# The V loads of an attention decode step, moved from SyncE's DMA queue to GpSimd's software queue

## The chip, the core and the metric

The kernel runs on one core of a Trainium2 chip. The metric is the time of one execution on the device in microseconds (us), the median of several runs; lower is better. A core has five engines that run side by side, each with its own instruction stream: TensorE (PE in the profile), VectorE (DVE), ScalarE (ACT), GpSimd (POOL) and SyncE (SP). Sixteen DMA engines move data between the memory of the chip and the core's on-chip memory; the instruction streams only issue the transfers.

## The reference

One decode step of attention for two sequences, gated by an MLP. All data are float32.

```python
def A(x, k_cache, v_cache, wq, wo):          # x [2, 1, 512]; caches [2, 32, 8192, 128]
    q = (x @ wq) split into 32 heads of 128
    scores = einsum("bhqd,bhkd->bhqk", q, k_cache) * 128 ** -0.5
    p = softmax(scores)
    o = einsum("bhqk,bhkd->bhqd", p, v_cache)
    return o joined over the heads @ wo      # wq [512, 4096], wo [4096, 512]

def B(x, w1, b1, w2, b2):
    return gelu(layernorm(x) @ w1 + b1) @ w2 + b2   # w1 [512, 1376], w2 [1376, 512]

xn = layernorm(x)
return x + A(xn, ...) * silu(B(xn, ...))
```

K and V together are 537 MB, each element of which is used once; the other inputs are 22 MB.

## The kernel before, in words

**Units.** The 64 pairs of sequence and head are taken two at a time: 32 units (n = 0 to 31). A unit needs 8.39 MB of K and as much of V, each laid out as 128 partitions of one contiguous row of 64 KB.

**Buffers.** There are three buffers of that size: two for K (`kb`, used in turn) and one for V (`vb`). They fill nearly all of the on-chip memory. `vb` is first used for the weights and scratch tiles of the MLP (the names in `boot`), and at the very end for `wo`; one of the `kb` first holds `wq`. The last unit's V goes into a K buffer, in two halves; K of the first and of the last unit come in two halves too.

**What a unit does.** VectorE multiplies K by the unit's query in two halves (L523, `scores_mul`, in place), sums the products over the 128 elements of a head in two halves (L530, `scores_sum`) and takes the maximum of each partition (L534). TensorE turns these maxima into a row (L537); VectorE takes the maximum of each of the two heads from it (L540, `max_dve`); TensorE spreads it again (L546), ScalarE copies it (L547) and computes the exponentials (L551) and a scaled column for the sums (L555). Then TensorE multiplies the exponentials with V in 32 steps (L574, `weighted`), ScalarE copies the sums (L581), TensorE folds them (L583) and VectorE writes them to the unit's columns of a table (L589, `spread`).

**The order of the units' work.** The loop at L594 writes the order out by hand for all engines, unit by unit, and each engine runs its own instructions in that order. For unit n it holds: first half of the multiply of n; the maximum of n-1 (L540) and its exponentials; second half of the multiply; `weighted(n-1)`; the load of V of n (`load_v`, L503); the sums and the maximum of n; `spread(n-1)`; the load of K of n+2 (`load_k`, L316). So on VectorE the maximum of unit n-1 stands behind the first multiply of unit n, and on SyncE, which issues both kinds of load, V of n stands ahead of K of n+2.

**The waits.** The class `Plan` records which instruction reads and writes which tile and puts the waits before the instructions. V of n waits until `weighted(n-1)` has read `vb`; K of n+2 waits until the sums of n (L530) have read its buffer. Every load has a semaphore for its kind and buffer. `load` (L313) issues all of them with SyncE's `dma_start`; only `x` (L339) is issued by ScalarE. The loads at the start are w1, w2, b1, b2, wq, K of unit 0 (two halves), K of unit 1 and V of unit 0; V of unit 0 waits until the MLP and the queries no longer need `vb`, K of unit 1 until `wq` has been used (L481). At the end `wo` comes in five pieces (L620) after the last use of `vb`, and is multiplied at L647 and L656.

**GpSimd** writes the identity matrix and three other constants at the start (L342 to L346) and has nothing else to do.

Of the kernel before, what the change touches and what calls it, by code (L numbers as in the profile page):

```python
# [21 lines left out]
class Plan:  # L22
# [18 lines left out]
    def op(self, eng, fn, r=(), w=(), over=(), it=None, loop=False, dma=None):  # L41


        o = Op()
        o.eng, o.fn, o.it, o.loop, o.dma, o.tell = eng, fn, it, loop, dma, False
        need = {}

        def after(d, war):
            if d.dma is None and dma is None and d.eng == eng and (eng == "pe" or war):
                return  # L50
            if d.dma is None:
                if need.get(d.eng) is None or need[d.eng].idx < d.idx:
                    need[d.eng] = d
            else:
                k = ("dma", d.dma)
                if need.get(k) is None or need[k].idx < d.idx:
                    need[k] = d

        for k in r:
            if k in self.writer:  # L60
                after(self.writer[k], False)
        for k in list(w) + list(over):
            if k in self.writer:
                after(self.writer[k], False)
            for d in self.readers.get(k, ()):
                after(d, True)
        clock = self.clock[eng]
        need = {k: d for k, d in need.items() if clock.get(k, 0) < d.idx}
        o.deps = [(k, d) for k, d in need.items()
                  if not any(e is not d and e.done.get(k, 0) >= d.idx for e in need.values())]  # L70
        for _, d in o.deps:
            for k, v in d.done.items():
                clock[k] = max(clock.get(k, 0), v)
        own = eng if dma is None else ("dma", dma)
        self.count[own] = o.idx = self.count.get(own, 0) + 1
        o.done = dict(clock)
        o.done[own] = o.idx
        for k in w:
            self.writer[k] = o
            self.readers[k] = []  # L80
        for k in r:
            if k not in w:
                self.readers.setdefault(k, []).append(o)
        self.ops.append(o)
# [80 lines left out]
def decode_kernel(nc, x, kc, vc, wq, wo, w1, b1, w2, b2, out):  # L165
# [31 lines left out]
    op = plan.op  # L197
# [13 lines left out]
    def sbuf(name, shape):  # L211
        return nc.alloc_sbuf_tensor(name, shape, F32).ap()
# [8 lines left out]
    vb = sbuf("vb", [P, KP * DH])  # L221
    kbuf = [t.rearrange("p (j d) -> p j d", d=DH) for t in kb]
    vbuf = vb.rearrange("p (j d) -> p j d", d=DH)
# [36 lines left out]
    boot = []  # L260
# [49 lines left out]
    vf = vc.rearrange("b h s d -> (b h s d)").rearrange("(n p j d) -> n p j d", p=P, j=KP, d=DH)  # L310
    M = KP // 2

    def load(dst, src, sem, w, over=()):  # L313
        op("sp", lambda: nc.sync.dma_start(dst, src), (), w, over=over, dma=sem)  # L314

    def load_k(n):  # L316
        i = (n + 1) % 2
        if n in (0, N - 1):
            for s in range(2):
                load(kbuf[i][:, s * M:(s + 1) * M], kf[n][:, s * M:(s + 1) * M], f"k{i}{s}", [("kb", i, s)])  # L320
            return
        load(kbuf[i], kf[n], f"kb{i}", [("kb", i, s) for s in range(2)])
# [4 lines left out]


    load(w1_sb, w1.rearrange("(p c) f -> p c f", p=P), "w1", ["w1"])
    load(w2_sb, w2.rearrange("f n -> (f n)").rearrange("(p e) -> p e", p=P), "w2", ["w2"])  # L330
    for t, src, k in ((b1_sb, b1, "b1"), (b2_sb, b2, "b2")):
# [169 lines left out]
    load_k(1)  # L501

    def load_v(n):  # L503
        load(vbuf, vf[n], "v", ["vb"], over=boot)

    load_v(0)

    def cols(t, a, n):
# [85 lines left out]
    for n in range(N):  # L594
        scores_mul(n, 0)
        if n:
            max_dve(n - 1)
            exps(n - 1)
        scores_mul(n, 1)

        if n:
            weighted(n - 1)
            if n < N - 1:
                load_v(n)
        scores_sum(n, 0)
        scores_sum(n, 1)
        max_rows(n)
        if n:
            spread(n - 1)

        if n + 2 < N:
            load_k(n + 2)
        elif n + 2 == N:
            for s in range(2):
                load(kbuf[1][:, s * M:(s + 1) * M], vf[N - 1][:, s * M:(s + 1) * M], f"v1{s}", [("kb", 1, s)])
# [80 lines left out]
```

## Time and profile before

| | |
|---|---|
| time, median of 3 runs | 1299.59 us (1299.52 to 1299.60) |
| span of the profiled execution, first to last instruction | 1298.3 us |
| moved by DMA | 559.39 MB, 431 GB/s over the span |
| VectorE busy | 1134.7 us (87%) |
| TensorE busy | 409.4 us (32%) |
| ScalarE busy | 77.6 us (6%) |
| GpSimd busy | 1.4 us |
| K load, issue to landing (median of 30) | 42.6 us |

The profile was taken in an execution of its own. Its span, 1298.3 us, runs from the first instruction to the last; the times of the runs contain what lies around that as well, and their median is 1.3 us longer. That table says who is busy, not who is waited for. For this the profile has a chain of waits (the work that ended last, followed back), a list of each engine's waits with what ended them, a timeline, and a table that gives each engine's busy time and the DMA engines' share in any stretch. An issue that waits in SyncE's stream shows as a wait of SPq, the queue of SyncE.

### The profile page before, as it was taken

Reading aid. Unit: us, or ns where it says so; the run is one execution under the profiler, and the core shown is the slowest. Engines: PE = TensorE matmul, PEld = TensorE weight load, DVE = VectorE, ACT = ScalarE, POOL = GpSimd, SP = SyncE. Lnnn points to the kernel's source line nnn. Section 1 sums busy time; section 2 is a strip of 40 time slices with the busy share of each in tenths; the row PEclk is TensorE's granted clock in tenths of the full one; section 3 lists DMA queues with packets and bytes.
Section 4 is the critical chain, followed back from the end, with each engine's and each line's share of the span. In section 5 each row is a group of like instructions: output and inputs, shape, how many; then the busy total and the mean of one; then the engine's idle time right before and its main releaser. Section 6 shows DMA issues by size and latency. Waiting matters only on the chain.

```text
span 1298.3 us, 6788 instructions
## 1 busy us (share of the span) xinstructions
PE 409.4 (32%) x2728; PEld 124.5 (10%) x2728; DVE 1134.7 (87%) x276; ACT 77.6 (6%) x250; POOL 1.4 (0%) x8
## 2 busy tenths in 40 slices
PE   5502333212333311333321333321333321333337
PEld 1100011000101000101100101000101100001103
DVE  3599989888889988889988888988888988888991
ACT  1100000000000000000000000000000000000000
POOL 0000000000000000000000000000000000000000
PEclk9856666556666556666555666655666655666659
DMA  9999999999999999999999999999999999999998
GB/s 406 445 423 444 424 436 436 426 444 426 440 428 430 440 426 444 424 436 436 426 444 426 440 428 434 438 424 444 426 434 436 426 444 426 440 428 434 423 436 360
DMA packets 10827, 559.39 MB, mean 431 GB/s; under 512 B 1208, under 2 KB 1216, under 8 KB 1476
## 3 DMA queue, kind: packets, MB, share of 16 engines
q1 hardware_dynamic: 10816, 559.30, 99.7%
q8 instruction: 4, 0.07, 0.0%
q14 instruction: 3, 0.02, 0.0%
q10 hardware_dynamic: 4, 0.00, 0.0%
HBM read 559.30 MB, written 0.00 MB: 431 GB/s over the span
## 4 chain that ended last, share of the span: by engine, by line
DMA 73%; PE 25%; DVE 1%; issue 0%; ACT 0%; SPq 0%; DVEq 0%
DMA vb<-in_A_v_cache_dram 71%; PE po L574 22%; DMA vb<-in_A_wo_dram 2%; PE s L409 1%; PE po L481 1%; PE s L451 0%; PE s L411 0%; PE acc L656 0%; DVE vb L417 0%; ACT L430 0%; DVE vb L355 0%; PE s L458 0%; SPq L314 0%; DVE vb L366 0%; DVE vb L443 0%
## 5 line engine op out<-in xcount | busy, mean ns | idle before, releaser
L523 DVE TENSOR_TENSOR kb<-kb,Q 128x8192 f32<-128x8192 f32 x64 | 555.6, 8681 | 106.3 <-DMA kb<-in_A_k_cache_dram 97.1
L530 DVE TENSOR_REDUCE sc<-kb 128x64 f32<-128x8192 f32 x64 | 552.3, 8666 | 0.0
L574 PE MATMUL po<-vb,PZ 128*8 128x512 f32 x1984 | 287.3, 744 | 296.4 <-DMA vb<-in_A_v_cache_dram 296.4
L546 PE MATMUL s<-nm,srow 1*128 1x2 f32 x64 | 18.4, 355 | 365.2 <-DVE nm L540 365.2
L574 PEld LDWEIGHTS po<-vb,PZ 128*8 128x8 f32 x1984 | 57.5, 104 | 500.2 <-issue 497.5
L537 PE MATMUL s<-ident,mx 128*1 128x128 f32 x32 | 11.8, 369 | 182.6 <-DVE mx L534 182.6
L546 PEld LDWEIGHTS s<-nm,srow 1*128 1x128 f32 x64 | 15.7, 302 | 374.5 <-DVE nm L540 374.5
L581 ACT COPY o<-po 128x512 f32<-128x512 f32 x32 | 18.7, 585 | 542.9 <-PE po L574 542.9
L547 ACT COPY bias<-s 128x2 f32<-128x2 f32 x32 | 5.1, 160 | 612.9 <-PE s L546 612.9
L583 PE MATMUL s<-mod,o 128*128 128x2 f32 x256 | 33.6, 253 | 22.1 <-ACT o L581 22.1
L583 PEld LDWEIGHTS s<-mod,o 128*128 128x128 f32 x256 | 31.1, 191 | 51.3 <-ACT o L581 51.3
L551 ACT ACTIVATE PZ<-sc,bias 64x128 f32<-64x128 f32 x64 | 25.5, 399 | 1.8
L537 PEld LDWEIGHTS s<-ident,mx 128*1 128x1 f32 x32 | 2.5, 79 | 186.1 <-DVE mx L534 155.5
L589 DVE TENSOR_TENSOR Z<-blk,s 128x8 f32 (+1 forms) x32 | 5.2, 163 | 12.4 <-PE s L583 12.4
L417 DVE COPY vb<-vb 2x384 f32<-2x384 f32 x4 | 1.8, 500 | 15.1 <-ACT vb L413 15.1
L551 ACT ACTIVATION_READ_ACCUMULATOR PZ<-sc,bias 64x1 f32 x64 | 11.8, 185 | 0.0
L409 PE MATMUL s<-vb 128*2 128x512 f32 (+1 forms) x24 | 11.7, 637 | 0.3 <-ACT vb L374 0.3
L665 DVE TENSOR_TENSOR gate<-acc,gate 128x128 f32<-128x128 f32 x1 | 0.3, 292 | 13.0 <-PE acc L656 13.0
L534 DVE TENSOR_REDUCE mx<-sc 128x1 f32<-128x128 f32 x32 | 9.2, 286 | 1.1
L555 ACT ACTIVATE ZR<-half,rs 128x8 f32 (+1 forms) x32 | 9.6, 301 | 4.1
L574 PE MATMUL po<-kb,PZ 128*8 128x512 f32 x64 | 8.7, 705 | 1.4 <-ACT PZ L551 1.4
L540 DVE TENSOR_REDUCE nm<-s 1x2 f32<-1x128 f32 x32 | 8.7, 272 | 0.3 <-PE s L537 0.3
(88 smaller groups left out, 83.8 us busy)
## 6 DMA issues: line engine op xcount, KB each, us to landing
kb<-in_A_k_cache_dram SPq DMA_DIRECT2D x4, 4096.0 KB, 43.3
kb<-in_A_v_cache_dram SPq DMA_DIRECT2D x2, 4096.0 KB, 40.5
vb<-in_B_w_dram SPq DMA_DIRECT2D x2, 2752.0 KB, 12.4
vb<-in_A_wo_dram SPq DMA_DIRECT2D x1, 4096.0 KB, 19.8
vb<-in_A_wo_dram SPq DMA_DIRECT2D x1, 2048.0 KB, 24.4
vb<-in_A_wo_dram SPq DMA_DIRECT2D x1, 1280.0 KB, 27.0
vb<-in_A_wo_dram SPq DMA_DIRECT2D x1, 512.0 KB, 27.7
vb<-in_A_v_cache_dram SPq DMA_DIRECT2D x31, 29.2
```

Of the source, the lines that this page charges most:

```text
L409: pe(lambda f=f, w=w, ph=ph, c=c: matmul(ph[:B, :w], yT[:, c, :], w1_sb[:, c, f:f + w], start=(c == 0), stop=False), ["yT", "w1"], [k])
L481: pe(lambda i=i, c=c, wv=wv, a=a, j=j, hd=hd: matmul(PO[R * j:R * j + NQ * B, :].rearrange("m (h d) -> m h d", d=DH), xnT[:, c, a:a + NQ * ...
L523: vector(n, n, lambda n: nc.vector.tensor_tensor(out=k, in0=k, in1=cols(Q, n * DH, DH).unsqueeze(1).to_broadcast([P, M, DH]), op=ALU.mult) ...
L530: vector(n, n, lambda n: nc.vector.tensor_reduce(out=SC[:, s * M:(s + 1) * M], in_=k, axis=AX.X, op=ALU.add), [("kb", i, s)], [("sc", s)])
L534: vector(n, n, lambda n: nc.vector.tensor_reduce(out=MX, in_=SC, axis=AX.X, op=ALU.max), [("sc", 0), ("sc", 1)], ["mx"])
L537: pe(lambda i: transpose(PM[:1, :P], MX, ident), ["mx", "ident"], ["s1"], it=n, loop=n > 0)
L546: pe(lambda i: matmul(PN[:, :U], srow, NM, start=True, stop=True), ["srow", "nm"], ["s2"], **one)
L551: act(lambda i, r=r, s=s: nc.scalar.activation(PZ[r, :, s, :], sc[r], AF.Exp, bias=BIAS[r, s:s + 1], scale=SCALE, accum_out=RS[r]), ["bias ...
L555: act(lambda i: nc.scalar.activation(cols(ZR, i * UP - UP, UP), half, AF.Copy, scale=RS), ["half"] + [("rs", s) for s in range(U)], [("ZR" ...
L574: pe(lambda i, t=t, j=j, v=v: matmul(PO[R * j:R * j + U * JW, :], PZ[:, t].rearrange("p s j -> p (s j)"), v[:, t * JW:(t + 1) * JW, :].rea ...
L581: act(lambda i: nc.scalar.copy(O4, PO), ["po"], ["o4"], **one)
L583: pe(lambda i, k=k: matmul(PT[:, :U], O4[:, k * DH:(k + 1) * DH], mod[:, k:U * JW:JW], start=(k == 0), stop=(k == JW - 1)), ["o4", "mod"], ...
```

## The change

V of units 0 to 30 is issued by GpSimd, over the queue whose descriptors a program on GpSimd writes (the software queue), instead of by SyncE over a hardware queue. `single_packet=True` asks that all that one DMA engine gets of such a load (eight rows of 64 KB) form one packet. The conditions of each load are the same as before; they stand in GpSimd's stream now. All K loads, the two halves of V of unit 31, the weights and `wo` stay on SyncE, in the order that they had among themselves. Nothing else differs; lines below the change move down by three.

```diff
-    def load(dst, src, sem, w, over=()):
-        op("sp", lambda: nc.sync.dma_start(dst, src), (), w, over=over, dma=sem)
+    def load(dst, src, sem, w, over=(), pool=False):
+        if pool:
+            op("pool", lambda: nc.gpsimd.dma_start(dst, src, single_packet=True), (), w, over=over, dma=sem)
+        else:
+            op("sp", lambda: nc.sync.dma_start(dst, src), (), w, over=over, dma=sem)
...
     def load_v(n):
-        load(vbuf, vf[n], "v", ["vb"], over=boot)
+        load(vbuf, vf[n], "v", ["vb"], over=boot, pool=True)
```

## Prediction

> **What bounds the kernel now.** I read the page's head first, its picture of the DMA engines and its queue table: 16 DMA engines at "9" in all but the last of 40 slices, and one queue, SyncE's, that fills 99.7% of their time.
>
> ```profile
> span 1298.3 us, 6788 instructions
> ...
> PE 409.4 (32%) x2728; PEld 124.5 (10%) x2728; DVE 1134.7 (87%) x276; ACT 77.6 (6%) x250; POOL 1.4 (0%) x8
> ...
> DMA  9999999999999999999999999999999999999998
> ...
> q1 hardware_dynamic: 10816, 559.30, 99.7%
> ```
>
> Then one unit in the middle of the run, from the table of stretches; the waits of SyncE's queue; and two neighbouring pieces of the chain of waits.
>
> ```profile
> 587.90:626.60 38.70, 10.73 (x75) 3.32 (x75) 35.03 (x8) 2.03 (x7) 0.00 (x0) 0.63 1.00 434
> ```
> ```profile
> SPq L314 <- PE po L574: 980.5, 31, 33.0
> SPq L314 <- DVE mx L534: 227.0, 31, 36.5
> ```
> ```profile
> 598.45 8.77 PE po L574 x64
> ...
> 637.14 9.90 PE po L574 x64
> ```
>
> From one V's first matmul to the next it is 637.14 - 598.45 = 38.7 us; in that unit the DMA share is 1.00 at 434 GB/s, while VectorE (third busy column) works 35.03 us. TensorE holds V's only buffer for some 9 us of it, and the DMA engines don't rest then: K is moving. Two equal loads, K and V of 8.39 MB, fill the unit, so one load takes 38.7 / 2 = **T = 19.35 us**, and each of the 8 rows of 64 KB that an engine carries of it (128 partitions over 16 engines) 2.42 us. The kernel is bound by the bytes. What a change adds is time in which the DMA engines have nothing to move; what it can save is their 0.3% of rest, at the ends.
>
> How the order in SyncE's queue keeps them busy stands in the timeline of that stretch, SyncE's issues first, then VectorE and one row of ScalarE (start, duration, engine, line; in brackets the idle time before).
>
> ```profile
> 607.24 0.33 SPq L314 DMA_DIRECT2D vb<-in_A_v_cache_dram  x1
> 613.82 0.33 SPq L314 DMA_DIRECT2D kb<-in_A_k_cache_dram  x1
> 647.06 0.33 SPq L314 DMA_DIRECT2D vb<-in_A_v_cache_dram  x1
> ```
> ```profile
> 617.84 8.69 DVE L523 TENSOR_TENSOR kb<-kb,Q 128x8192 f32<-128x8192 f32 x1 [3.64 <-DMA kb<-in_A_k_cache_dram]
> 626.45 0.27 DVE L540 TENSOR_REDUCE nm<-s 1x2 f32<-1x128 f32 x1
> 626.65 8.67 DVE L523 TENSOR_TENSOR kb<-kb,Q 128x8192 f32<-128x8192 f32 x1
> 635.25 17.26 DVE L530 TENSOR_REDUCE sc<-kb 128x64 f32<-128x8192 f32 x2
> 652.54 0.29 DVE L534 TENSOR_REDUCE mx<-sc 128x1 f32<-128x128 f32 x1
> 652.78 0.16 DVE L589 TENSOR_TENSOR Z<-blk,s 128x8 f32 x1
> ```
> ```profile
> 628.41 0.18 ACT L551 ACTIVATION_READ_ACCUMULATOR PZ<-sc,bias 64x1 f32 x1
> ```
>
> When V is issued at 607.24, the K load ahead of it has 617.84 - 607.24 = 10.6 us to go. That K lands, VectorE starts on it, V follows (637.14), then the K issued at 613.82. Every load queues behind one under way, and the half-finished one is always completed first.
>
> For later: VectorE's unit is 652.78 + 0.16 - 617.84 = **35.1 us**. From a unit's first multiply to the weights of the unit before (its maximum, L540, stands behind that multiply) it is 628.41 + 0.18 - 617.84 = **10.8 us** with the hand-over. TensorE holds V for 647.06 - 637.14 = 9.92 us here and for 607.24 - 598.45 = 8.79 before, mean **9.36 us**.
>
> **The change part by part.** 31 V loads leave SyncE's queue (0.33 us of issue each, off the path) and become 31 DMA instructions on GpSimd, which has nothing else left to do (8 instructions, 1.4 us in all). Bytes and compute stay. The waits stay too, but no longer in one line: K(n+2) isn't issued behind V(n), nor does V(n) move behind K(n+1). So the price hangs on how a DMA engine shares its time between two queues. The trace shows that in one place, the start.
>
> ```profile
> 0.73 0.87 SPq L314 DMA_DIRECT2D vb<-in_B_w_dram  x2
> ...
> 0.89 0.54 ACTq L339 DMA_DIRECT2D vb<-in_A_x_dram  x1
> ...
> 5.23 0.62 DVE L361 BATCH_NORM_STATS2 vb<-vb 2x6 f32<-2x512 f32 x1
> ```
> ```profile
> vb<-in_B_w_dram SPq DMA_DIRECT2D x2, 2752.0 KB, 12.4
> ```
>
> x (4 KB, ScalarE's queue) is issued after w1 and in use at 5.23. w1's 2752 KB at 434 GB/s take 6.5 us, so w1 was not through before 7.2. x got in between w1's rows: a hardware queue's load can be cut at a row, and then the other queue has its turn. By this a V whose eight rows are one packet waits for the K row under way, then has the engines for 19.35 us, while **K(n+1), half done, stands**. The sum is made for that. The Trainium skill ("DMA: Bandwidth & Descriptors", Queues, rings and completion order) says that an engine takes its queues in turn and changes only at the end of a packet; by that V runs through uncut, as here. It also calls packets of 9 to 17 descriptors typical, by which a K load might be one packet too and nothing would be reordered: rival 2. x among w1's rows speaks against that.
>
> *The software queue's delay* **L** (V issued to V moving, and its last byte to TensorE's start) isn't in the trace. The nearest row is the store at the end, on the hardware queue and nearly without bytes:
>
> ```profile
> 1296.51 0.66 SPq L667 DMA_DIRECT2D out_dram<-gate  x1
> ```
> ```profile
> 1.16 0.29 POOL L343 TENSOR_SCALAR_AFFINE_SELECT ident<-ident 128x128 f32<-128x128 f32 x1 [0.23 <-POOL ident L342]
> ```
>
> From its issue to the span's end it is 1298.3 - 1296.5 = 1.8 us, the lower end. The upper end is x's 5.23 - 0.89 = 4.3 us, which holds a row's wait. I take the nearer row and one small GpSimd instruction (0.29) on top: L = 2.1 us. The same page of the Trainium skill puts the software queue's first byte 0.4 us behind the hardware queue's; by that L would be 2.2 and the sum 1 us more.
>
> *Steady state.* Let an odd unit's multiply start at 0, its K just landed, the next K buffer full or taken. The weights of the unit before are ready at 10.8; its V, in place since long, is read until 20.2; there the next V is issued, and it moves 2.1 us later. The DMA engines have meanwhile moved one K (19.35 from 0) and then had nothing: both K buffers full, V's being read. They rest 20.2 + 2.1 - 19.35 = **2.9 us**. VectorE is through at 35.1 and a K is issued, which starts when V is done. The even unit's V is ready 35.1 us after the odd one's, so 35.1 - 19.35 = 15.75 us into that K; it cuts it with 3.6 us to go (a row begun and one whole) and delays it by 19.35. VectorE waits for it some 10 us, and then starts an odd unit again; this wait costs nothing more, the engines move bytes in it. A pair of units takes 2 x 38.7 + 2.9. Units 3 to 30 are 14 pairs: 14 x 2.9 = **+41 us**.
>
> *Start.*
> ```profile
> 45.66 0.43 SPq L314 DMA_DIRECT2D vb<-in_A_v_cache_dram  x1
> ```
> ```profile
> 47.74 17.38 DVE L523 TENSOR_TENSOR kb<-kb,Q 128x8192 f32<-128x8192 f32 x2 [8.24 <-ACT Q L496]
> 65.03 17.27 DVE L530 TENSOR_REDUCE sc<-kb 128x64 f32<-128x8192 f32 x2
> ```
> w1, w2, wq and K0 (22.4 MB, 51.6 us at 434 GB/s) are in at about 54. V0, issued at 45.66, now cuts in ahead of K0's second half, which comes at 54 + 19.35 = 73.4; unit 0 ends at 73.4 + 8.7 + 17.3 = 99.4 instead of 65.03 + 17.27 = 82.3, and K2 is issued there. K1 is in at 93, so the engines rest 7 to 8 us. V1 is issued at 99.4 + 20.2, again some 1.5 us late: together **+10 us**.
>
> *End.*
> ```profile
> 1268.16 0.29 DVE L534 TENSOR_REDUCE mx<-sc 128x1 f32<-128x128 f32 x1
> ```
> ```profile
> 1285.50 3.66 PE L647 MATMUL wide<-vb,on 128*17 128x512 f32 x32 [0.47 <-DMA vb<-in_A_wo_dram]
> 1290.40 1.94 PE L647 MATMUL wide<-vb,on 128*17 128x512 f32 x16 [1.25 <-DMA vb<-in_A_wo_dram]
> 1293.49 1.31 PE L656 MATMUL acc<-vb,on 128*17 128x128 f32 x40 [1.15 <-DMA vb<-in_A_wo_dram]
> ```
> Now unit 31's maximum is done early and the end waits for wo, last at 1293.5. V30 will cut ahead of K31's second half; after that half only V31 and wo (8.39 MB each, 38.7 us) remain, so it lands at 1293.5 + 41 + 10 - 38.7 = 1305.8. Then come 8.7 + 17.3 us of VectorE, and from the maximum on the stretch of now without its waits for wo (0.47 + 1.25 + 1.15): 1298.3 - 1268.2 - 2.9 = 27.2. The span ends at 1359.0, which is 1359.0 - 1298.3 - 51 = **+10 us** more.
>
> Sum: 1298.3 + 41 + 10 + 10 = 1359; the median of the runs, 1299.59, lies 1.3 us over this span, so **1361 us**.
>
> **Rivals.** *1. The packet isn't kept whole* (the change doesn't do what it says): rows of V and K take turns. A V beside a whole K takes 15 rows and L, 36.3 + 2.1; TensorE 9.36; the next V meets a K that has moved alone for 11.5 us, 19.35 + 7.9 + 2.1; TensorE 9.36: 86.5 us a pair, 9.1 over 77.4. 14 x 9.1 and some 3 at the start: **1430 us** (1414 to 1446, since TensorE's 8.8 to 9.9 counts twice a pair). For it: x and w1 took turns. Against: V's rows are asked for as one packet.
>
> *2. On the other side: K's loads can't be cut.* If a load of 64 KB rows holds an engine to its end, V waits for K(n+1) as now and still comes ahead of K(n+2): 10.6 us of cover against L. Price nothing, **1299.6**, if at the start K1 goes ahead of V0; with V0 first, K1 lands at 93 and the engines rest once, some 4 us: 1303. It decides where an engine is committed to 10.6 us of K, over four rows. x's place speaks against it, though w1's rows are a third as long.
>
> *3. V comes too late to cut.* The margin is 3.6 - 2.42 = 1.2 us, and TensorE's times differ by as much from V to V: in some units K finishes first and the rest falls away. Half of them would make it 1340; it lies in the range.
>
> *4. VectorE holds up GpSimd.* If descriptors could be written only between two VectorE instructions, each V issued at 20.2 would wait for the reduction that ends at 26.1: 14 x 5.9 more, **1444 us**. The Trainium skill ("SBUF — State Buffer", SBUF: two separate sides) has such a lock for VectorE's two-port modes; L523's 8192 elements in 8.69 us, less than one a nanosecond, don't look like one.
>
> **How the numbers follow.** Forecast 0.55, with rival 3 from 1335 to 1392 (L from 1.8 to 4.3: 1357 to 1392; TensorE at 8.8 or 9.9: 8 us either way); rival 1 0.20; rival 2 0.10, half of it no change; rival 4 0.05; 0.10 for what I don't see, of it 0.03 faster and 0.01 the same. Faster has only the 0.3% of rest to live on. The range that leaves out 2 in 10 is 1330 to 1445: forecast, rival 1 and rival 4. Within 0.2% (2.6 us), about what a measurement of this kernel can tell from no change: 0.06; faster 0.03; slower 0.91.
>
> **What would show it.** The page's table of DMA issues gives the time from a V's issue to its landing now:
>
> ```profile
> vb<-in_A_v_cache_dram SPq DMA_DIRECT2D x31, 29.2
> ```
>
> Right: a GpSimd queue with 260 MB beside the hardware queue's 299; V issued to landed in some 21 to 24 us instead of 29.2; VectorE waiting for K every second unit, some 10 us; DMA rests of 3 us at every second unit. Rival 1: V in 29 to 38 us, and TensorE waiting for V. Rival 2: VectorE's wait at 3.6 us a unit as now, DMA at "9" throughout. Wrong altogether: V's rows slower than 2.42 us, or GpSimd issuing V well after TensorE's last matmul on it.

## The result, and the profile after

| | time, median | runs |
|---|---|---|
| before | 1299.57 us | 1299.52 to 1299.60 (4) |
| changed | 1441.09 us | 1440.65 to 1442.87 (4) |

The ratio is 1.1092, 95% interval 1.1078 to 1.1105: 141.5 us slower, where 61 us were forecast. The sign and the cause in the large (DMA engines at rest between loads) were forecast; the way to it was rival 1's, not the forecast's. The time lies inside the stated range, 1330 to 1445 us, only because that range was drawn wide enough to hold rivals 1 and 4. The time alone can't tell these two apart (1430, up to 1446, and 1444 us); the traces and runs below do.

From the page after, the lines that answer to those of before:

```profile
span 1439.3 us, 6789 instructions
...
PE 397.9 (28%) x2728; PEld 122.5 (9%) x2728; DVE 1136.4 (79%) x276; ACT 77.7 (5%) x250; POOL 18.0 (1%) x39
...
DMA  9999999989979899798899988898989898899995
...
q1 hardware_dynamic: 6352, 299.25, 49.3%
q0 software_dynamic: 4464, 260.05, 41.8%
```

VectorE's and TensorE's busy times are as they were. The DMA engines are not: 49.3 + 41.8 = 91.1% of 1439.3 us is 1311 us with a packet on, against 99.7% of 1298.3, 1294 us, before. So of the 141 us that the span grew, 128 - 4 = **124 us are rest**, and 17 us are packets that took longer.

V's time from issue to landing, and TensorE's wait for V (before, after), are the signs that the prediction had named:

```profile
vb<-in_A_v_cache_dram POOLq DMA_DIRECT2D x31, 33.6
```
```profile
PE po L574 <- DMA vb<-in_A_v_cache_dram: 296.4, 31, 13.5
PE po L577 <- DMA vb<-in_A_v_cache_dram: 638.5, 30, 27.8
```

The landing's median was 29.2 us before. The forecast had 21 to 24 us for it, rival 1 had 29 to 38 and TensorE waiting for V. Both of rival 1's signs are there.

One V load in the middle, its TensorE work and the next, from the chain of waits; then VectorE's timeline and the issues of K and V in the same stretch:

```profile
634.19 32.61 DMA vb<-in_A_v_cache_dram
666.80 0.12 issue
666.92 9.89 PE po L577 x64
676.82 0.28 issue
677.10 34.65 DMA vb<-in_A_v_cache_dram
```
```profile
635.80 0.16 DVE L592 TENSOR_TENSOR Z<-blk,s 128x8 f32 x1 [9.96 <-PE s L540]
635.95 8.69 DVE L526 TENSOR_TENSOR kb<-kb,Q 128x8192 f32<-128x8192 f32 x1
...
670.66 0.29 DVE L537 TENSOR_REDUCE mx<-sc 128x1 f32<-128x128 f32 x1
678.68 0.16 DVE L592 TENSOR_TENSOR Z<-blk,s 128x8 f32 x1 [7.74 <-PE s L540]
```
```profile
670.65 0.33 SPq L317 DMA_DIRECT2D kb<-in_A_k_cache_dram  x1
```

V's issue to the next V's issue is 42.9 us here, and 43.5 on average from unit 2 to unit 30; before it was 38.7 on average (38.1 or 39.8 from one to the next). V takes 32.6 and 34.7 us to land here; V's landing and TensorE's work on it make up the whole unit, since the next V needs the same buffer. VectorE stands idle 10 and 8 us at the end of these two units ahead of L592, the small write of V's result, because that V is late (the bracket names TensorE's L540, which TensorE runs behind V's last step). Held there, VectorE starts the next unit late, and the K load that needs this unit's buffer is issued late, at 670.65.

What the DMA engines do between the V issue at 634.19 and that K issue is shown by the table of queues, in three stretches: 634.2 to 638.9, 641.5 to 655.9, and 666.5 to 671.5.

```profile
DMA packets 32, 2.10 MB, mean 446 GB/s; under 512 B 0, under 2 KB 0, under 8 KB 0
## 3 DMA queue, kind: packets, MB, share of 16 engines
q1 hardware_dynamic: 32, 2.10, 103.1%
```
```profile
q1 hardware_dynamic: 48, 3.15, 50.4%
q0 software_dynamic: 48, 3.15, 50.4%
```
```profile
DMA packets 0, 0.00 MB, mean 0 GB/s; under 512 B 0, under 2 KB 0, under 8 KB 0
```

In the first stretch K alone moves, two rows on each of 16 engines, though V has been issued. In the second both queues move the same, three rows each per engine. In the third nothing moves: V's last row is in, and the next K is issued only at 670.65. Laid end to end by their times in the trace, the 64 KB packets of each of the 16 engines from 626.5 to 666 us read the same (k is a row of K, V one of V):

```
kkkkkVkVkVkVVVVV
```

In this stretch V's rows are not run through together while K has rows left. A whole unit's rows are there, 16 x 2.42 = 38.7 us, and then the rest.

### The profile page after: what moved, and what is told of

Read it like the earlier page. It is cut to its first block, busy times and chain, and to the rows that moved or that the text cites. A ratio compares the mean times of both kernels' runs of the same rounds, so it can differ in the third digit from the quotient of the medians.

```text
span 1439.3 us, 6789 instructions
## 1 busy us (share of the span) xinstructions
PE 397.9 (28%) x2728; PEld 122.5 (9%) x2728; DVE 1136.4 (79%) x276; ACT 77.7 (5%) x250; POOL 18.0 (1%) x39
## 3 DMA queue, kind: packets, MB, share of 16 engines
q1 hardware_dynamic: 6352, 299.25, 49.3%
q0 software_dynamic: 4464, 260.05, 41.8%
## 4 chain that ended last, share of the span: by engine, by line
DMA 74%; PE 23%; issue 2%; ACT 0%; DVE 0%; SPq 0%; DVEq 0%
DMA vb<-in_A_v_cache_dram 70%; PE po L577 20%; DMA kb<-in_A_k_cache_dram 3%; DMA vb<-in_B_b_dram 1%; PE po L484 0%; PE s L412 0%; PE s L454 0%; PE wide L650 0%; PE s L564 0%; PE s L414 0%; PE s L586 0%; PE acc L659 0%; DVE vb L420 0%; ACT PZ L554 0%; PE s L426 0%
## 5 line engine op out<-in xcount | busy, mean ns | idle before, releaser
L577 PE MATMUL po<-vb,PZ 128*8 128x512 f32 x1984 | 282.4, 733 | 639.8 <-DMA vb<-in_A_v_cache_dram 638.5
L592 DVE TENSOR_TENSOR Z<-blk,s 128x8 f32 (+1 forms) x32 | 5.2, 163 | 236.1 <-PE s L540 217.6
L586 PE MATMUL s<-mod,o 128*128 128x2 f32 x256 | 33.6, 253 | 22.1 <-ACT o L584 22.1
L315 POOL DMA_DIRECT2D vb<-in_A_v_cache_dram x31 | 16.6, 535 | 1352.2 <-PE po L577 1261.0
L540 PE MATMUL s<-ident,mx 128*1 128x128 f32 x32 | 9.0, 282 | 67.1 <-DVE mx L537 67.1
L554 ACT ACTIVATE PZ<-sc,bias 64x128 f32<-64x128 f32 x64 | 25.5, 399 | 1.8
L543 DVE TENSOR_REDUCE nm<-s 1x2 f32<-1x128 f32 x32 | 8.7, 272 | 0.0
L540 PEld LDWEIGHTS s<-ident,mx 128*1 128x1 f32 x32 | 2.7, 85 | 68.2 <-issue 35.9
## 6 DMA issues: line engine op xcount, KB each, us to landing
vb<-in_A_v_cache_dram POOLq DMA_DIRECT2D x31, 33.6
```

Source lines behind the costliest of these rows:

```text
L315: op("pool", lambda: nc.gpsimd.dma_start(dst, src, single_packet=True), (), w, over=over, dma=sem)
L540: pe(lambda i: transpose(PM[:1, :P], MX, ident), ["mx", "ident"], ["s1"], it=n, loop=n > 0)
L554: act(lambda i, r=r, s=s: nc.scalar.activation(PZ[r, :, s, :], sc[r], AF.Exp, bias=BIAS[r, s:s + 1], scale=SCALE, accum_out=RS[r]), ["bias ...
L577: pe(lambda i, t=t, j=j, v=v: matmul(PO[R * j:R * j + U * JW, :], PZ[:, t].rearrange("p s j -> p (s j)"), v[:, t * JW:(t + 1) * JW, :].rea ...
L586: pe(lambda i, k=k: matmul(PT[:, :U], O4[:, k * DH:(k + 1) * DH], mod[:, k:U * JW:JW], start=(k == 0), stop=(k == JW - 1)), ["o4", "mod"], ...
```

## The experiments

**Theory 1**: an engine gives two queues one row each by turns, whether one packet was asked for or not and whatever the kind of queue. V lands late, VectorE waits for it, the next K is issued late, and the engines rest. **Theory 2**: the software queue is slow. **Theory 3**: the request for one packet holds rows together at least partly. Where a control is named, the run is read against it.

**Without the request for one packet.**
```diff
-            op("pool", lambda: nc.gpsimd.dma_start(dst, src, single_packet=True), (), w, over=over, dma=sem)
+            op("pool", lambda: nc.gpsimd.dma_start(dst, src), (), w, over=over, dma=sem)
```


> The changed kernel without the request for one packet (single_packet left out). Theory 1 (the DMA engines give the two queues one 64 KB row each by turns, whatever the request): nothing changes, 1434 to 1448 us, V's issue to landing 33 to 34 us. Theory 3 (the request does hold part of V's rows together): V's rows are cut up more, and the time moves by more than 1%.

Measured: 1445.28 us (ratio 1.112, 1.1102 to 1.1139), V's landing 33.7 us. The intervals of the run with the request and of this one touch; the request does nothing that can be told here.

**K on the software queue, V on the hardware queue.**
```diff
-        load(vbuf, vf[n], "v", ["vb"], over=boot, pool=True)
+        load(vbuf, vf[n], "v", ["vb"], over=boot)
...
-        load(kbuf[i], kf[n], f"kb{i}", [("kb", i, s) for s in range(2)])
+        load(kbuf[i], kf[n], f"kb{i}", [("kb", i, s) for s in range(2)], pool=True)
```


> Swapped queues: K of units 1 to 30 over GpSimd's software queue, V over SyncE's hardware queue. Theory 1 (turns between any two queues): 1415 to 1450 us, V lands 31 to 35 us after its issue as in the changed kernel. Theory 2 (the software queue itself is slow, some 4.4 us per load: its descriptors, its issue): V is quick again, K has more time to spare, and the time falls to 1300 to 1360 us.

Measured: 1447.56 us (1.1138, 1.1116 to 1.1161). The page's table of issues of this run:

```profile
vb<-in_A_v_cache_dram SPq DMA_DIRECT2D x31, 34.3
kb<-in_A_k_cache_dram POOLq DMA_DIRECT2D x30, 34.2
```

V is as late over the hardware queue as over the software queue, and the time is not the 1300 to 1360 us of theory 2. Two queues cost this, whichever of them V is in.

**Everything in the one software queue**, in SyncE's old order (K from unit 1 on, V, and wo).
```diff
-            load(kbuf[i], kf[n], ...)   # the same for K's halves of unit 31, V's halves, and wo
+            load(kbuf[i], kf[n], ..., pool=True)
```


> Every load from K of unit 1 on (K, V, wo) over GpSimd's one software queue, in SyncE's old order. Theory 1: with one queue there is nothing to take turns with, and the order of before is back: 1299 to 1305 us. Theory 2 (slow software queue): 62 loads at some 4.4 us or more, 1441 us or above.

Measured: 1306.85 us (1.0046, 1.0028 to 1.0064), 2 us over the range expected. Two stretches of it, the first 100 us and the steady part (DMA share and GB/s are the last columns):

```profile
0.00:100.00 100.00, 37.40 (x193) 10.43 (x193) 48.80 (x54) 12.14 (x25) 3.12 (x11) 0.74 0.95 403
237.24:1227.45 990.21, 284.33 (x1894) 85.73 (x1898) 899.51 (x182) 52.17 (x181) 27.44 (x52) 0.61 1.00 433
```

In the steady part the software queue keeps the engines at 1.00 and 433 GB/s, just as SyncE's queue did before in that stretch. The 7 us are lost at the start, where the first stretch has a share of 0.95 (before 0.99): V of unit 4 is issued at 227.82, before at 220.87, and the profiled span is 8.1 us longer (1306.4 us), so only 1 us is lost after that. K of unit 0 is still in SyncE's queue there, beside the loads of GpSimd's; that this is what costs the 7 us was not tried by itself. With one queue the order is back, and all but 7 of the 141 us are gone. That is far from theory 2's 1441 us or above: theory 2 falls.

**VectorE's write of V's result moved** behind the next unit's first multiply (the table Z gets one unit of columns in front, so that the loop stays regular).
```diff
         scores_mul(n, 0)
         if n:
+            spread(n - 2)
             max_dve(n - 1)
...
-        if n:
-            spread(n - 1)
```


> The changed kernel, with VectorE's small write that needs V's result (spread of unit n-1) moved behind the first multiply of unit n+1, so that VectorE no longer waits for V at the end of a unit. Theory 1 (V's late landing costs time because VectorE waits for it and so issues the next K late, while the DMA engines rest): most of the loss goes, 1318 to 1350 us. Rival (the alternation itself makes the transfers slower): 1425 to 1445 us.

Measured: 1372.01 us (1.0557, 1.0536 to 1.0578): half of the loss goes, 69 us, not most of it, and the time is 22 us over the range expected. The alternation alone would have left it at 1425 or more, so the wait is real; that the rest stays has its reason in VectorE's own list of waits:

```profile
DVE Z L592 <- PE s L540: 143.0, 17, 12.7
```

VectorE still waits in about every second unit (17 times), now behind the first multiply. The row names L592, which stands there directly ahead of the maximum of the unit before (L543); the transpose for that maximum, L540, stands on TensorE behind all 32 steps on V. V's lateness reaches VectorE by this way too; my expectation had left that out.

> Control: the kernel before with VectorE's write of V's result moved behind the next unit's first multiply. V is in time there, so nothing should change: 1298 to 1302 us.

The same edit of the kernel before: 1299.57 us (1.0000, 0.9989 to 1.0011). The edit is worth nothing by itself.

**K in four loads, rows of 16 KB.**
```diff
-        load(kbuf[i], kf[n], f"kb{i}", [("kb", i, s) for s in range(2)])
+        for r in range(4):
+            a = r * KP // 4
+            load(kbuf[i][:, a:a + KP // 4], kf[n][:, a:a + KP // 4], f"kb{i}{r}", [("kq", i, r)],
+                 over=[("kb", i, r // 2)])
...
-            [("kb", i, s)] + qs, [("kb", i, s)])
+            [("kb", i, s), ("kq", i, 2 * s), ("kq", i, 2 * s + 1)] + qs, [("kb", i, s)])
```


> The changed kernel with K of units 1 to 30 in four loads each, so that SyncE's rows are 16 KB and V's on GpSimd's queue stay 64 KB. Theory 1 (one row each by turns, whatever its size): V gets four fifths of each engine while K is there, lands in 22 to 28 us instead of 33.6, and the time falls to 1310 to 1365 us. Rival (the two queues share by bytes or by time, or the software queue is slow): V still lands after 33 to 34 us, 1430 to 1450 us.

> Control: the kernel before, with K of units 1 to 30 in the same four loads each, all on SyncE's queue. All theories: 1299 to 1304 us, so that what the run with quarter rows on two queues shows comes from the sharing.

Measured: 1317.98 us (1.0147, 1.013 to 1.0164); the control 1306.71 (1.0056, 1.0036 to 1.0076), 3 us over the range expected, so four loads of short rows cost 7 us by themselves and the second queue 11. Its row for V in the table of issues, and its steady part:

```profile
vb<-in_A_v_cache_dram POOLq DMA_DIRECT2D x31, 28.5
```
```profile
237.00:1227.00 990.00, 281.03 (x1890) 84.53 (x1894) 889.02 (x181) 52.12 (x181) 13.20 (x25) 0.61 1.00 431
```

V lands 5 us sooner (28.5, half a us outside what was expected), the engines are at 1.00 again, and the time is 123 us shorter; against the control, 130 of the 141 us are gone. While both queues have rows, the trace has one for one: from 625.5 to 635 us each queue starts 48 packets, V's of 64 KB and K's of 16 KB. But the edit does more than shorten K's rows. Each quarter of K is now a load with a wait of its own: two quarters of a K are issued when half of the sums that free the buffer are done (581.48 and 581.85, the other two at 590.07 and 590.44), and VectorE begins a unit when half of its K is in. So V's earlier landing goes with the shorter turns, but how much of the 123 us is due to them and how much to the earlier K was not separated.

**V in pieces of 16 KB**, as one packet and not.
```diff
-            op("pool", lambda: nc.gpsimd.dma_start(dst, src, single_packet=True), (), w, over=over, dma=sem)
+            op("pool", lambda: nc.gpsimd.dma_start(dst, src, single_packet=True, max_dma_last_dim=16384), (), w, over=over, dma=sem)
```

The second run has `max_dma_last_dim=16384` alone.

> The changed kernel with each V row cut into four pieces of 16 KB, still one load and one packet per engine asked for; K's rows stay 64 KB. Theory 1 (a turn is one piece of a load, the request for one packet does not hold pieces together): V gets one fifth of an engine while K is there, lands after 36 to 44 us on a median, 1435 to 1475 us. Theory 3 (the request holds, but only pieces under 64 KB): V runs through uncut, lands in 21 to 25 us, 1340 to 1385 us.

> The same with V's rows cut into pieces of 16 KB, without the request for one packet. Theory 1: as with the request, within 1%: 1435 to 1475 us. Theory 3: 1435 to 1475 us too, that is 5% or more above the run with the request.

Measured: 1466.46 us (1.1285, 1.1262 to 1.1308) with the request, 1467.56 (1.1293, 1.1271 to 1.1316) without: the same. Theory 3 falls for small pieces too. The times are in the range expected; V's landing is not, 33.6 and 32.4 us against the 36 to 44 expected. K, with four fifths of each engine, lands in 25.5 us instead of 33.9, and V has the engines alone after that. While both have pieces left, each queue gets as many turns as the other, with the request for one packet in place (655 to 673.5 us, V's queue is q0):

```profile
q1 hardware_dynamic: 96, 6.29, 78.4%
q0 software_dynamic: 96, 1.57, 19.8%
```

**K in pieces of 4 KB**, so that V gets nearly all of an engine: what the forecast had assumed.
```diff
-            op("sp", lambda: nc.sync.dma_start(dst, src), (), w, over=over, dma=sem)
+            op("sp", lambda: nc.sync.dma_start(dst, src, max_dma_last_dim=cut), (), w, over=over, dma=sem)
...
-        load(kbuf[i], kf[n], f"kb{i}", [("kb", i, s) for s in range(2)])
+        load(kbuf[i], kf[n], f"kb{i}", [("kb", i, s) for s in range(2)], cut=4096)
```


> The changed kernel with K's rows of units 1 to 30 cut into pieces of 4 KB (one load each, as before), so that V gets 16 of 17 turns by bytes while K is there: nearly what the forecast assumed, V through uncut. V should land 23 to 26 us after its issue. If the forecast's sum was right apart from that premise: 1345 to 1375 us plus what the control loses. If a V that comes early does little harm, as with quarter rows: 1305 to 1330 us plus what the control loses.

> Control: the kernel before with K's rows of units 1 to 30 cut into pieces of 4 KB, all on SyncE's queue. 1300 to 1330 us, by what small pieces cost; the run with the 4 KB pieces on two queues is read against this one.

Measured: 1378.50 us (1.0608, 1.0577 to 1.0638); the control 1333.41 (1.0261, 1.0231 to 1.029), 3 us over the range expected. Here only the size of K's pieces differs, not the loads or their waits. V's landing, and the packets from 571 to 588 us, where V's 64 KB rows and K's 4 KB pieces take turns one for one:

```profile
vb<-in_A_v_cache_dram POOLq DMA_DIRECT2D x31, 25.1
```
```profile
q0 software_dynamic: 112, 7.34, 99.8%
q1 hardware_dynamic: 112, 0.46, 6.7%
```

A turn is one piece, whatever its size. Against the control the loss is 45 us, the lower edge of what was expected if the forecast's sum held (45 to 75), where that sum has 61. Two waits of VectorE and the issues of V:

```profile
578.99 0.16 DVE L592 TENSOR_TENSOR Z<-blk,s 128x8 f32 x1
591.03 8.69 DVE L526 TENSOR_TENSOR kb<-kb,Q 128x8192 f32<-128x8192 f32 x1 [11.87 <-DMA kb<-in_A_k_cache_dram]
...
625.97 0.16 DVE L592 TENSOR_TENSOR Z<-blk,s 128x8 f32 x1
626.13 8.69 DVE L526 TENSOR_TENSOR kb<-kb,Q 128x8192 f32<-128x8192 f32 x1
```
```profile
564.90 0.53 POOL L315 DMA_DIRECT2D vb<-in_A_v_cache_dram  x1 [35.78 <-PE po L577]
610.57 0.53 POOL L315 DMA_DIRECT2D vb<-in_A_v_cache_dram  x1 [45.14 <-PE po L577]
646.89 0.53 POOL L315 DMA_DIRECT2D vb<-in_A_v_cache_dram  x1 [35.79 <-PE po L577]
```

This is the schedule of the forecast: V in time (no wait at L592), K delayed in every second unit (11.87 us), then none, and a pair of units of 82.0 us. The control's span is 1332.0 - 1298.2 = 33.8 us over that of before, about 1.1 us a unit, so its pair is near 79.6: 2.4 us of loss per pair where the forecast has 2.9. V lands soonest of all runs on two queues here, and yet 45 us are lost against the control, where the run with K in four loads loses 11: now K is what comes late.

## Why the prediction was wrong, point by point

- **The bound** was right: the bytes, and most of the loss is rest of the DMA engines (124 of 141 us).
- **The step that failed** is "By this a V whose eight rows are one packet waits for the K row under way, then has the engines for 19.35 us". The first half of what it rests on was right (a load can be cut at a row; x had shown it). The second took the request for one packet at its word. The runs show turns of one row with the request and without, at 64 KB and at 16 KB, and V lands 33.6 us after its issue instead of 21 to 24. In the sum it is the term of the steady state: 14 x 2.9 = 41 us were forecast, and from V of unit 2 to V of unit 30 it is 14 x 9.6 = 134 us (151.85 to 1370.42, before 142.92 to 1227.45). The trace before had more of this than the forecast read from it: on x's queue two packets of 2 KB begin at 2.99 and 3.10 and two of 4 bytes at 4.02 and 4.04, and rows of w1 of 0.83 us, begun at 3.20 and 3.21, fit exactly in between. By these times x's own load was cut after one row as well, on a hardware queue and without a request for one packet. The forecast gave the turns 0.20.
- **Rival 1**'s 1430 us were 11 us short. Its pair of 86.5 us is 87.0 on average over those 14 pairs (single ones differ, 588.74 to 677.10 is 88.4): 7 us in all. 6 more are lost at the start, 9 us by V of unit 2 where it had some 3, and the end gains 2. One thing that it lacked shows in the trace: V's turn comes later, since with K under way two whole K rows go first (the stretch to 638.9 above), where the prediction counted the row under way alone.
- **Where the loss enters** was only half seen. Rival 1 had TensorE waiting for V. That VectorE waits for V too, by L592 and by TensorE's order, wasn't in its sum; the moved write shows the wait at L592 to be worth 69 of 141 us. How the other 72 divide between TensorE's order and the single V buffer was not tried.
- **L**, 2.1 us, had little to do with the time: the swap moves V to a hardware queue and the time stays. At rest V's first row begins 1.2 us after the issue (below). With turns, a V that starts later finds fewer K rows left; that is argued, not tried.
- **The start**: V of unit 2, behind which the 14 pairs lie, is issued 9 us late (forecast 10), V of unit 4 16 us late (237.24, before 220.87). **The end** loses nothing (forecast 10): from the last V issue on GpSimd's queue, 1370.42, to the end of the span are 68.9 us, before 1298.3 - 1227.45 = 70.9.
- **Rival 2** (loads that can't be cut) and **rival 4** (VectorE holding GpSimd up) are excluded, the one by the turns, the other by the swap and by the single software queue at 433 GB/s. Against rival 4 there is also the V issued at 115.02: its first row starts by 116.3, while VectorE is in the sums that begin at 112.52 and take 8.7 us each. Rival 3 was part of the forecast's schedule and had no place.
- **The 17 us of longer packets** go with the pauses. By the packets' times in the trace, 15 of them are in the first row that an engine moves after a rest: 368 such rows, 23 an engine, of 3.06 us on average instead of 2.42. Why a first row takes longer was not tested.

## What to carry to other kernels

Where the DMA engines are the bound, the order of the loads in one queue is a resource: each load is completed before the next takes bytes from it. A second queue gives that order up, and then the size of the other queue's rows decides how late a load lands: V landed after 33.6, 28.5 and 25.1 us beside K's rows of 64, 16 and 4 KB. What one load gains the other loses: with the soonest V, K came late in every second unit, and 45 us were still lost. Before loads are split over queues, look for a load whose lateness holds up the engine that issues or frees the next one.

## What the runs showed of the hardware that was not expected

- The request for one packet had no effect on the turns, at 8 pieces of 64 KB per engine (1441.1 with, 1445.3 without) and at 32 of 16 KB (1466.5 and 1467.6).
- The software queue is no slower than the hardware queue in the steady state: 433 GB/s and a share of 1.00, with one instruction of 0.53 us on GpSimd per load.
- With the engines at rest, V's first row starts 1.2 us after an issue at 115.02; no packet starts from 115.1 to 116.2. With K under way it starts some 5 us after the issue at 634.19, behind two whole rows of K. This lead of K does not go by the number of rows: with K in 4 KB pieces V's first row still starts 3.8 us after the issue at 564.90 (370 packets of K and none of V up to 568.6), with K's rows of 16 KB 3.6 us after the issue at 611.58. Less the 1.2 us, that leaves some 2.5 us of K as an estimate, about one row of 64 KB, or 16 pieces of 4 KB.
- Short rows have a price on a single queue: K in four loads with rows of 16 KB costs 7 us (0.6%), K in pieces of 4 KB 34 us (2.6%), for half of the bytes.
